# Top-32 attention and a low-rank mixer in one kernel: a fold's maximum read from PSUM, keys stored tail first, and weighted values at the head of a step

## The chip, the cores and the metric

The kernel runs on one core of one Trainium2 chip. The core has a matrix engine (TensorE, PE in the profile, with its weight loader PEld), three other compute engines (VectorE or DVE, ScalarE or ACT, GpSimd or POOL) and a queue engine (SyncE, SP) that issues most transfers here. Each engine runs its own instructions in order; semaphores tie them together. The metric is the time of one execution on the device in microseconds, as a median of several. For the kernel before that is 1749.21 us (three runs, 1747.92 to 1749.37).

## The reference, cut to what matters

There are 8 batches, 8 heads, 576 positions and head dimension 64, all in float32. The outputs of the heads of a batch, side by side, are the input of a mixer of 512 channels.

```python
scores = scale * np.matmul(q, k.transpose(0, 1, 3, 2))          # 576 x 576 per head
kth = np.partition(scores, -32, axis=-1)[..., -32:-31]
scores = np.where(scores >= kth, scores, -1e9)
attn = exp(scores - max) / (sum + 1e-9)
x = matmul(attn, v)                       # heads side by side: (8, 576, 512)
h = x.transpose(0, 2, 1) @ U @ V          # rank 32, over positions
u = x + h.transpose(0, 2, 1)
out = u + np.maximum(u @ w_ch1, 0.0) @ w_ch2    # 512 -> 2048 -> 512
```

The costly part outside the matrix products is the 32nd largest of 576 scores in each row.

## The kernel before, in words

**Groups and steps.** Two heads of one batch make a group g (0 to 31, four to a batch). A group has five query tiles t: four of 128 rows (t = 0 to 3, "full tiles"), in which both heads have 128 rows each, and a tail tile (t = 4) in which the last 64 rows of both heads share the 128 partitions. Step n is group n // 5, tile n % 5; there are 160. One Python loop (L753 to L866) writes out the order of all engines by hand, without a scheduler. In step n it issues the scores of step n+1, most of the top-32 search of step n, the transposes of the weights of step n-1, and the weighted values of an earlier step. Steps from 21 on use the second half of the loop's body (L830 on).

**Scores.** `scores` (L310) makes a full tile's scores in two PSUM tiles, `scs[0]` and `scs[1]`, each two banks wide: `scs[0]` has the first 288 keys of head 0 and of head 1, `scs[1]` the other 288. The products have a contraction of 64, so that the two heads use the two halves of the PE array (shown as 64*128 in the profile). The PSUM pool `ps_s` has two buffers. ScalarE copies the scores to SBUF with three instructions (L346 to L348), because in SBUF a row is [head 0: main 512, tail 64][head 1: tail 64, main 512], while the keys lie main first for both heads. `load` (L237) reads keys in that order with one transfer for the main part and one for the tail of each block. From group 5 on (`blocked`, L279) inputs are loaded in blocks of 32 and turned by VectorE's transpose (L290) rather than by PE.

**Top 32 with a fold.** From group 4 on, a row of 576 scores is folded in two halves of 288: `upper` has the larger of each pair, `lower` the smaller. GpSimd adds the two halves as integers (stage 0, L370), VectorE takes the maximum (stage 1, L372), and GpSimd subtracts it from the sum (L373), which leaves the smaller one exactly. `fold` starts this right after the scores, `split` does the second stage some way later in the same step. VectorE then looks for maxima in `lower` (L412 to L416) and in `upper` (L426, L438, L443).

**Weights and values.** After the top 32 is known, ScalarE and GpSimd drop the other scores and ScalarE takes the exponential (L377). From step 30 on the weights of a full tile are transposed by VectorE in blocks of 32 (L498) and by way of DRAM (`away`, L504, then one transfer L508 into `PT`, which has two buffers); the last piece goes through PE (L531). `values` (L541) multiplies the transposed weights with v on PE: for a full tile one product over the whole array (L560) and eight that use half the array's columns (L564, shown as 128*64), for a tail tile five over the whole array (L550). ScalarE copies the result (L573; L558 for a tail tile, after VectorE's reciprocal of the sums, L539). In step n these are the values of step n-2, in the middle of the step (L850 to L853). When a group's tail tile has had its values, `mixed` is queued for that group (transposes, the low-rank products), and after four groups the batch's MLP becomes a filler.

**Filler.** The MLP of the batch before (L633, L652: 256 products of 256 or 320 columns) fills PE during the attention of the next. `fill` (L725) is called eight times a step; each call adds a fixed share to an account `due` and issues MLP products until that is spent, or sets it to zero if no MLP is queued. For steps up to 42 the share is multiplied by 0.91 (`EARLY`). What is left of the last MLPs runs after the last step.

Of the kernel before, what the change touches and what calls it, by code (L numbers as in the profile page):

```python
# [12 lines left out]
ALU = mybir.AluOpType  # L13
# [13 lines left out]
def kernel(  # L27
# [28 lines left out]
    nc = tc.nc  # L56
    B, H, S, D = q.shape
# [5 lines left out]
    NT, TAIL = 4, 64  # L63
    MAIN = NT * P
    HALF = S // 2
# [4 lines left out]
    CH = NT + 1  # L70
    ALONE = NPAIR * CH
# [4 lines left out]
    BLK = 32  # L76
# [52 lines left out]
    def cols(t):  # L129
        return slice(t * P, t * P + rows(t))  # L130
# [4 lines left out]
    def half(h):  # L135
        return slice(h * D, (h + 1) * D)
# [77 lines left out]
    raws, parts, passes = [], [], []  # L214
# [17 lines left out]


    raw, qkTs, S2s, uTs, XTs, dens = {}, {}, {}, {}, {}, {}
    probs, PTs, folds = {}, {}, {}

    def load(g):  # L237
        b, h0 = g // NPAIR, 2 * (g % NPAIR)
        ld = loads.tile([P, 2 * S], F32, tag="ld", name="ld")
        if blocked(g):  # L240
            for i, src in enumerate((q, k)):
                for a in range(4):
                    ds = src[b, h0 + a // 2, :, a % 2 * BLK : (a % 2 + 1) * BLK]
                    to = ld[a * BLK : (a + 1) * BLK, i * S : (i + 1) * S]
                    nc.sync.dma_start(
                        to[:, 0:MAIN].rearrange("i (t m d) -> i t m d", t=NT, d=BLK),
                        ds[0:MAIN].rearrange("(m i t) d -> i t m d", i=BLK, t=NT),
                    )
                    nc.sync.dma_start(
                        to[:, MAIN:S].rearrange("i (m d) -> i m d", d=BLK),  # L250
                        ds[MAIN:S].rearrange("(m i) d -> i m d", i=BLK),
                    )
            raw[g] = ld
        else:
            tiles = []
            ends = ld[:, 2 * MAIN : 2 * S].rearrange("p (h d) -> p h d", h=2)
            for j, src in enumerate((q, k)):
                t = ld[:, j * MAIN : (j + 1) * MAIN].rearrange("p (t h d) -> p t h d", t=NT, h=2)
                for i in range(2):
                    queue = nc.scalar if g == 0 and i else nc.sync  # L260
                    queue.dma_start(
                        t[:, :, i, :],
                        src[b, h0 + i, 0:MAIN, :].rearrange("(p t) d -> p t d", t=NT),
                    )
                tiles.append(t)
            for i, src in enumerate((q, k)):
                nc.sync.dma_start(
                    ends[half(i)], src[b, h0 : h0 + 2, MAIN:S, :].rearrange("h p d -> p h d")
                )
            raw[g] = tiles, ends  # L270
        va, vd, vt = (a[g % NV] for a in (vas, vds, vts))
        for i in range(2):
            nc.sync.dma_start(
                va[:, i], v[b, h0 + i, 0:MAIN, :].rearrange("(p t) d -> p t d", t=NT)
            )
            nc.sync.dma_start(vd[half(i), half(i)], v[b, h0 + i, MAIN:S, :])
        nc.sync.dma_start(vt[TAIL:P], v[b, h0 : h0 + 2, MAIN:S, :].rearrange("h p d -> p h d"))

    def blocked(g):  # L279

        return g > NPAIR
# [26 lines left out]
    def scores(g, t):  # L310

        qkT = qkTs[g]
        S2 = attn.tile([P, 2 * (S + TAIL)], F32, tag="Ssb", name="Ssb", bufs=4)
        n = 2 if t < NT else 1
        probs[g, t] = S2
        S2s[g, t] = S2[:, 0 : n * S].rearrange("p (c n) -> p c n", c=n)
        if t == NT:
            sc = ps_s.tile([P, 2, 512], F32, tag="sc", name="sc")  # L320
            for i in range(2):
                for h in range(2):
                    nc.tensor.matmul(  # L323
                        sc[half(h), i, 0:HALF],
                        lhsT=qkT[half(h), 0, cols(t)],
                        rhs=qkT[half(h), 1, i * HALF : (i + 1) * HALF],
                        start=True,
                        stop=True,
                    )
            nc.scalar.copy(S2[:, 0:S].rearrange("p (i n) -> p i n", i=2), sc[:, :, 0:HALF])  # L330
            return
        scs = [ps_s.tile([P, 2, 512], F32, tag="sc", name="sc") for _ in range(2)]
        for i, sc in enumerate(scs):
            for h in range(2):
                nc.tensor.matmul(  # L335
                    sc[:, h, 0:HALF],
                    lhsT=qkT[half(h), 0, cols(t)],
                    rhs=qkT[half(h), 1, i * HALF : (i + 1) * HALF],
                    start=True,
                    stop=True,  # L340
                )

        main = S2.rearrange("p (h n) -> p h n", h=2)
        last = S2[:, MAIN : MAIN + 2 * TAIL].rearrange("p (h n) -> p h n", h=2)
        copy = nc.vector.tensor_copy if g + t == 0 else nc.scalar.copy
        copy(main[:, :, 0:HALF], scs[0][:, :, 0:HALF])  # L346
        nc.scalar.copy(main[:, :, HALF:MAIN], scs[1][:, :, 0 : MAIN - HALF])
        nc.scalar.copy(last, scs[1][:, :, MAIN - HALF : HALF])  # L348

    def fold(g, t):  # L350

# [11 lines left out]
    def pair(g, t, stage):  # L363
        S2 = S2s[g, t]
        n = S2.shape[1]
        upper, lower = folds[g, t]
        top, bottom = upper[:, 0:n, 0:HALF], lower[:, 0:n].bitcast(U32)
        a, b = S2[:, :, 0:HALF], S2[:, :, HALF:S]
        if stage == 0:
            nc.gpsimd.tensor_tensor(bottom, a.bitcast(U32), b.bitcast(U32), ALU.add)  # L370
        else:
            nc.vector.tensor_tensor(top, a, b, ALU.max)  # L372
            nc.gpsimd.tensor_tensor(bottom, bottom, top.bitcast(U32), ALU.subtract)  # L373

    def weigh(chunk, E, nmax, total=None):
# [165 lines left out]
    def values(g, t):  # L541

        PT = PTs.pop((g, t))
        va, vd, vt = (a[g % NV] for a in (vas, vds, vts))
        O = ps_t.tile([P, P], F32, tag="tp", name="O")
        if t == NT:
            den, x = dens[g], xs[g % 2]
            inverse(g, 2 * NT if g == NPAIR - 1 else 0, 2 * NT + 1)
            for j in range(NT + 1):
                nc.tensor.matmul(  # L550
                    O,
                    lhsT=PT[:, j],
                    rhs=va[:, :, j, :] if j < NT else vt,
                    start=(j == 0),
                    stop=(j == NT),
                )
            for h in range(2):
                nc.scalar.mul(x[half(h), NT, half(h)], O[half(h), half(h)], den[half(h), 2 * NT :])  # L558
            return
        nc.tensor.matmul(O, lhsT=vd, rhs=PT[:, 2 * NT], start=True, stop=False)  # L560
        PB = PT[:, 0 : 2 * NT].rearrange("p (a h) (c j) -> p h c a j", h=2, c=NT)
        for j in range(NT):
            for h in range(2):
                nc.tensor.matmul(  # L564
                    O[half(h)],
                    lhsT=va[:, h, j, :],
                    rhs=PB[:, h, j] if shared(g, t) else PT[:, NT * h + j],
                    start=False,
                    stop=(j == NT - 1),
                )  # L570
        if t == 0:
            XTs[g] = attn.tile([P, MAIN], F32, tag="XT", name="XT")
        nc.scalar.copy(XTs[g][:, cols(t)], O)  # L573
# [144 lines left out]
    STEPS = NP * CH  # L718
# [6 lines left out]
    def fill(k=1):  # L725


        nonlocal due
        for _ in range(k):
            if passes:  # L730
                passes.pop(0)()
            if mixing and next(mixing[0], True):
                mixing.pop(0)
            due += share * (SHORT if t == NT else 1) * (EARLY if n <= 2 * ALONE + 2 else 1)
            while due > 0:
                if not fillers:
                    due = 0.0
                    break
                done = next(fillers[0], None)
                if done is None:  # L740
                    fillers.pop(0)
                else:
                    due -= done

    load(0)
    next_params(1)
    t = 0
# [5 lines left out]
    for n in range(STEPS + 2):  # L753
# [77 lines left out]
        if ease:  # L831
            next(last, None)
        fill()
        if n + 1 < STEPS:
            scores(*divmod(n + 1, CH))
            fold(*divmod(n + 1, CH))
# [10 lines left out]
        next(here, None)  # L847
        next_params(1)
        fill()
        if n - 2 >= ALONE:  # L850
            values(*divmod(n - 2, CH))
            if (n - 2) % CH == NT:
                mixing.append(mixed((n - 2) // CH, 5))  # L853
        next(here, None)
        split(*divmod(n + 1, CH))
        if away:
# [43 lines left out]
```

## Time and profile before

| | |
|---|---|
| median of the runs | 1749.21 us |
| the profiled execution | 1745.95 us |
| its span, from first to last instruction | 1744.1 us |
| attention of groups 0 to 3, no filler yet | until about 215 us |
| attention with filler | 215 to some 1612 us |
| last batch's MLP alone | 1612 to 1744 us |
| mean clock granted to PE | 0.968 (0.78 until 215 us, 1.00 from 320 on) |
| HBM | 95 GB/s over the span |

How to read it: an engine's busy time is what its instructions cover; idle time on an engine that is not the bottleneck costs nothing, and which engine is the bottleneck differs from stage to stage. A 4-byte matrix product appears as two records on PE and two on its weight loader. The number after the shape, 64*128 or 128*64, is the part of the array that a product uses. In a line of a group, the figures after the bar are busy time, mean length of one in ns, and the engine's idle time before them with what ended it.

### The profile page before, as it was taken

Reading aid. Unit: us, or ns where it says so; the run is one execution under the profiler, and the core shown is the slowest. Engines: PE = TensorE matmul, PEld = TensorE weight load, DVE = VectorE, ACT = ScalarE, POOL = GpSimd, SP = SyncE. Lnnn points to the kernel's source line nnn. Section 1 sums busy time; section 2 is a strip of 40 time slices with the busy share of each in tenths; the row PEclk is TensorE's granted clock in tenths of the full one; section 3 lists DMA queues with packets and bytes.
Section 4 is the critical chain, followed back from the end, with each engine's and each line's share of the span. In section 5 each row is a group of like instructions: output and inputs, shape, how many; then the busy total and the mean of one; then the engine's idle time right before and its main releaser. Section 6 shows DMA issues by size and latency. Waiting matters only on the chain.

```text
span 1744.1 us, 29711 instructions
## 1 busy us (share of the span) xinstructions
PE 1638.1 (94%) x9435; PEld 1202.4 (69%) x9435; DVE 1515.5 (87%) x4358; ACT 1030.4 (59%) x2690; POOL 973.2 (56%) x759
## 2 busy tenths in 40 slices
PE   4576789999999999999999999999999999999999
PEld 2444556677667776678767776678767776678677
DVE  7999889899999999999999999999999999993000
ACT  4888787665656666565656656565656666563100
POOL 4778787656555555656555555656555555652000
PEclk7678899999999999999999999999999999999999
DMA  3332222344444443444444444444444444422010
GB/s 89 89 93 82 71 72 60 70 111 112 112 109 122 107 117 101 116 107 112 109 111 120 103 113 106 116 113 112 109 112 123 105 111 105 121 85 82 3 16 13
DMA packets 275837, 167.36 MB, mean 96 GB/s; under 512 B 173920, under 2 KB 260192, under 8 KB 275680
## 3 DMA queue, kind: packets, MB, share of 16 engines
q1 hardware_dynamic: 274624, 165.20, 36.4%
q8 instruction: 74, 1.21, 0.3%
q14 instruction: 83, 0.68, 0.1%
q10 hardware_dynamic: 1056, 0.26, 0.1%
HBM read 101.42 MB, written 63.96 MB: 95 GB/s over the span
## 4 chain that ended last, share of the span: by engine, by line
PE 73%; DVE 16%; ACT 3%; DMA 3%; POOL 3%; issue 2%; SPq 1%; POOLq 0%; DVEq 0%; ACTq 0%
PE mm L652 26%; PE mm L633 23%; PE sc L335 6%; PE O L564 6%; DVE m L443 5%; DVE hT L438 3%; DVE upper L438 2%; DMA PT<-away 2%; PE sc L323 2%; DVE first L426 2%; PE O L550 2%; PE up L608 1%; PE tp L531 1%; PE O L560 1%; PE tp L526 1%
## 5 line engine op out<-in xcount | busy, mean ns | idle before, releaser
L652 PE MATMUL mm<-hT,w 128*128 128x256 f32 (+1 forms) x2048 | 544.6, 410 | 0.7 <-ACT hT L645 0.7
L633 PE MATMUL mm<-uT,w 128*128 128x256 f32 (+1 forms) x2048 | 540.2, 411 | 0.0
L471 POOL TENSOR_TENSOR Ssb<-Ssb,E 128x576 f32<-128x576 f32 x271 | 379.4, 1418 | 270.5 <-ACT E L468 269.9
L633 PEld LDWEIGHTS mm<-uT,w 128*128 128x128 f32 x2048 | 376.1, 192 | 100.0 <-issue 13.3
L652 PEld LDWEIGHTS mm<-hT,w 128*128 128x128 f32 x2048 | 373.6, 192 | 95.2 <-issue 11.7
L443 DVE MAX8 m<-upper 128x8 f32<-128x304 f32 x756 | 323.9, 466 | 2.9
L373 POOL TENSOR_TENSOR lower<-lower,upper 128x576 uint32<-128x576 uint32 (+1 forms) x140 | 180.5, 1289 | 137.2 <-DVE upper L372 130.5
L377 ACT ACTIVATE Ssb<-Ssb,nmax 128x576 f32<-128x576 f32 x286 | 222.6, 783 | 17.2 <-POOL Ssb L448 9.2
L370 POOL TENSOR_TENSOR lower<-Ssb 128x576 uint32<-128x576 uint32 (+1 forms) x140 | 194.8, 1392 | 59.3 <-DVE first L426 18.3
L438 DVE MATCH_REPLACE8 upper<-m,upper 128x304 f32<-128x304 f32 x504 | 227.6, 459 | 0.0
L645 ACT ACTIVATE hT<-mm 128x320 f32<-128x320 f32 (+1 forms) x256 | 105.8, 413 | 201.1 <-PE mm L633 198.7
L468 ACT ACTIVATE E<-Ssb,least 128x576 f32<-128x576 f32 x271 | 197.9, 769 | 5.2
L335 PE MATMUL sc<-qkT 64*128 64x288 f32 x1024 | 167.7, 448 | 9.3 <-ACT Ssb L346 8.5
L564 PE MATMUL O<-PT,va 128*64 128x128 f32 x2048 | 144.4, 285 | 9.8 <-DMA PT<-away 9.5
L498 DVE STREAM_TRANSPOSE y<-Ssb 128x512 f32<-128x512 f32 x208 | 138.5, 694 | 8.2 <-ACT Ssb L377 7.4
L335 PEld LDWEIGHTS sc<-qkT 64*128 64x128 f32 x1024 | 91.9, 194 | 71.3 <-issue 27.8
L412 DVE MAX8 upper<-lower 128x8 f32<-128x288 f32 x252 | 103.0, 445 | 41.0 <-POOL lower L373 41.0
L372 DVE TENSOR_TENSOR upper<-Ssb 128x576 f32<-128x576 f32 (+1 forms) x140 | 123.7, 884 | 11.6 <-ACT Ssb L348 11.0
L564 PEld LDWEIGHTS O<-PT,va 128*64 128x64 f32 x2048 | 113.0, 140 | 27.0 <-DMA PT<-away 12.2
L665 DVE TENSOR_TENSOR oT<-uT,mm 128x320 f32<-128x320 f32 (+1 forms) x8 | 3.6, 455 | 140.8 <-PE mm L652 140.8
L346 ACT COPY Ssb<-sc 128x576 f32<-128x576 f32 x127 | 80.6, 635 | 71.4 <-PE sc L335 69.9
L573 ACT COPY XT<-O 128x128 f32<-128x128 f32 x128 | 34.2, 267 | 143.1 <-PE O L564 143.1
(95 smaller groups left out, 2233.8 us busy)
## 6 DMA issues: line engine op xcount, KB each, us to landing
away<-y SPq DMA_DIRECT2D x416, 128.0 KB, 2.4
PT<-away SPq DMA_DIRECT2D x104, 512.0 KB, 3.3
raw<-in_moe_w_ch_dram SPq DMA_DIRECT2D x32, 512.0 KB, 3.8
va<-in_v_dram SPq DMA_DIRECT2D x64, 128.0 KB, 2.2
out_dram<-ob SPq DMA_DIRECT2D x57, 128.0 KB, 2.0
ld<-in_q_dram SPq DMA_DIRECT2D x108, 64.0 KB, 2.6
ld<-in_k_dram SPq DMA_DIRECT2D x108, 64.0 KB, 2.3
ld<-in_q_dram SPq DMA_DIRECT2D x108, 8.0 KB, 2.2
```

Of the source, the lines that this page charges most:

```text
L335: nc.tensor.matmul(sc[:, h, 0:HALF], lhsT=qkT[half(h), 0, cols(t)], rhs=qkT[half(h), 1, i * HALF : (i + 1) * HALF], start=True, stop=True,)
L370: nc.gpsimd.tensor_tensor(bottom, a.bitcast(U32), b.bitcast(U32), ALU.add)
L373: nc.gpsimd.tensor_tensor(bottom, bottom, top.bitcast(U32), ALU.subtract)
L377: nc.scalar.activation(E, chunk, AF.Exp, bias=nmax, scale=SCALE, accum_out=total)
L438: nc.vector.match_replace(nxt, ms[c], curs[c], NEG)
L443: nc.vector.max(ms[c], curs[c])
L468: nc.scalar.activation(gap, chunks[c], AF.Relu, bias=least[:, c : c + 1], scale=-WIDEN)
L471: nc.gpsimd.tensor_tensor(chunks[c], chunks[c], gap, ALU.subtract)
L498: nc.vector.transpose(y[:, :, h].rearrange("p r c j -> p c r j"), E2[:, a : a + MAIN].rearrange("p (c r j) -> p c r j", c=NT, r=4),)
L564: nc.tensor.matmul(O[half(h)], lhsT=va[:, h, j, :], rhs=PB[:, h, j] if shared(g, t) else PT[:, NT * h + j], start=False, stop=(j == NT - 1),)
L633: nc.tensor.matmul(ph[:, 0:w], lhsT=w1[:, cc, f * P : (f + 1) * P], rhs=uT[:, cc, lo:hi], start=(cc == 0), stop=(cc == NC - 1),)
L652: nc.tensor.matmul(po[:, 0:w], lhsT=w2[:, f, c * P : (c + 1) * P], rhs=hTs[f][:, 0:w], start=(f == 0), stop=(f == NF - 1),)
```

## The change

Three things are changed together.

- For blocked groups (5 to 31) the keys of head 1 are loaded tail first: [tail 64, main 512]. Head 1's two parts of 288 are then already in the order in which SBUF has them. A full tile's `scs[0]` gets part 0 of head 0 and part 1 of head 1, `scs[1]` the other two, and ScalarE makes two copies of 2 x 288 instead of three. For the tail tile the scores keep their order, so that one of its four products becomes two (224 and 64 columns).
- The fold's maximum takes one of its two operands from the PSUM tile (`fronts_of`) and not from its copy in SBUF: for full tiles of blocked groups, and for all tail tiles. GpSimd's addition reads SBUF as before. The PSUM tile is in use until the maximum has read it.
- The values of step n-3 are issued at the head of step n, directly before the scores of step n+1, in place of those of step n-2 in the middle of the step. Only the last two steps keep the old place. `mixed` is queued from there too.

```diff
     def load(g):
...
+                    lead = TAIL if i and a >= 2 else 0
                     nc.sync.dma_start(
-                        to[:, 0:MAIN].rearrange("i (t m d) -> i t m d", t=NT, d=BLK),
+                        to[:, lead : lead + MAIN].rearrange("i (t m d) -> i t m d", t=NT, d=BLK),
                         ds[0:MAIN].rearrange("(m i t) d -> i t m d", i=BLK, t=NT),
                     )
+                    end = 0 if lead else MAIN
                     nc.sync.dma_start(
-                        to[:, MAIN:S].rearrange("i (m d) -> i m d", d=BLK),
+                        to[:, end : end + TAIL].rearrange("i (m d) -> i m d", d=BLK),
                         ds[MAIN:S].rearrange("(m i) d -> i m d", i=BLK),
                     )
...
     def scores(g, t):
...
+        def product(out, h, lo, hi):
+            nc.tensor.matmul(
+                out,
+                lhsT=qkT[half(h), 0, cols(t)],
+                rhs=qkT[half(h), 1, lo:hi],
+                start=True,
+                stop=True,
+            )
+
         if t == NT:
             sc = ps_s.tile([P, 2, 512], F32, tag="sc", name="sc")
             for i in range(2):
                 for h in range(2):
...
+                    lo = i * HALF + (TAIL if h and blocked(g) else 0)
+                    hi = min(lo + HALF, S)
+                    product(sc[half(h), i, 0 : hi - lo], h, lo, hi)
+                    if hi - lo < HALF:
+                        product(sc[half(h), i, hi - lo : HALF], h, 0, TAIL)
             nc.scalar.copy(S2[:, 0:S].rearrange("p (i n) -> p i n", i=2), sc[:, :, 0:HALF])
+            fronts_of[g, t] = sc[:, 0:1, 0:HALF]
             return
...
         for i, sc in enumerate(scs):
             for h in range(2):
...
+                part = 1 - i if h and blocked(g) else i
+                product(sc[:, h, 0:HALF], h, part * HALF, (part + 1) * HALF)
+        if blocked(g):
+            for i, sc in enumerate(scs):
+                nc.scalar.copy(ends_of(S2, i), sc[:, :, 0:HALF])
+            fronts_of[g, t] = scs[0][:, :, 0:HALF]
+            return
...
+    def ends_of(S2, i):
+
+        parts = S2[:, 0 : 4 * HALF].rearrange("p (a n) -> p a n", a=4)
+        return parts[:, 1:3] if i else parts[:, 0:4:3]
+
...
     def pair(g, t, stage):
...
         a, b = S2[:, :, 0:HALF], S2[:, :, HALF:S]
+        if t < NT and blocked(g):
+            a, b = (ends_of(probs[g, t], i) for i in range(2))
...
-            nc.vector.tensor_tensor(top, a, b, ALU.max)
+            nc.vector.tensor_tensor(top, fronts_of.pop((g, t), a), b, ALU.max)
...
+    def weighted(m):
+
+        values(*divmod(m, CH))
+        if m % CH == NT:
+            mixing.append(mixed(m // CH, 5))
...
         if ease:
             next(last, None)
         fill()
+        if ALONE <= n - 3 <= STEPS - 3:
+            weighted(n - 3)
         if n + 1 < STEPS:
             scores(*divmod(n + 1, CH))
             fold(*divmod(n + 1, CH))
...
         fill()
-        if n - 2 >= ALONE:
-            values(*divmod(n - 2, CH))
-            if (n - 2) % CH == NT:
-                mixing.append(mixed((n - 2) // CH, 5))
+        if n >= STEPS:
+            weighted(n - 2)
         next(here, None)
         split(*divmod(n + 1, CH))
```

In it `P` is 128, `S` 576, `NT` 4, `CH` 5, `MAIN` 512, `TAIL` 64, `HALF` 288, `ALONE` 20 and `STEPS` 160.

More of the change, by code (lines that the diff above doesn't have):

```diff
@@ L234 @@
     raw, qkTs, S2s, uTs, XTs, dens = {}, {}, {}, {}, {}, {}
-    probs, PTs, folds = {}, {}, {}
+    probs, PTs, folds, fronts_of = {}, {}, {}, {}
     def load(g):
@@ L322, in scores @@
                 for h in range(2):
[L323 to L329, printed above, removed]
+                    lo = i * HALF + (TAIL if h and blocked(g) else 0)
[3 more added lines that the diff above has]
+                        product(sc[half(h), i, hi - lo : HALF], h, 0, TAIL)
             nc.scalar.copy(S2[:, 0:S].rearrange("p (i n) -> p i n", i=2), sc[:, :, 0:HALF])
+            fronts_of[g, t] = sc[:, 0:1, 0:HALF]
             return
@@ L334, in scores @@
             for h in range(2):
[L335 to L341, printed above, removed]
+                part = 1 - i if h and blocked(g) else i
[5 more added lines that the diff above has]
+            return
         main = S2.rearrange("p (h n) -> p h n", h=2)
```

## The prediction

> **What bounds the kernel now.** I read the page's busy times first, then busy time by stage, then the waits and the groups by shape in the stages that matter, and last TensorE's timeline of one step with the chain of waits. The page alone leaves two candidates:
>
> ```profile
> PE 1638.1 (94%) x9435; PEld 1202.4 (69%) x9435; DVE 1515.5 (87%) x4358; ACT 1030.4 (59%) x2690; POOL 973.2 (56%) x759
> ```
>
> Busy time by stage (columns: stretch, its length, then busy time of PE, weight loader, VectorE, ScalarE, GpSimd, clock, DMA share, GB/s):
>
> ```profile
> 215.00:446.00 231.00, 214.05 (x1248) 154.79 (x1247) 217.13 (x630) 155.25 (x394) 156.92 (x121) 0.97 0.34 88
> 446.00:1577.00 1131.00, 1127.34 (x6627) 829.01 (x6627) 1082.05 (x3259) 690.40 (x1851) 656.25 (x507) 1.00 0.43 111
> 1577.00:1612.00 35.00, 34.27 (x215) 29.36 (x215) 9.86 (x26) 12.31 (x34) 8.51 (x9) 1.00 0.25 72
> 1612.00:1744.00 132.00, 126.68 (x525) 98.66 (x523) 7.03 (x15) 14.62 (x36) 0.72 (x1) 0.99 0.06 11
> ```
>
> From 446 to 1577 us PE is busy 1127.3 of 1131 and VectorE 1082: PE binds, with VectorE only 49 us behind. Before 446 PE idles 17 us and VectorE 14. After 1612 there is only the last batch's MLP on PE. A busy PE need not be a full one, so I ask who waited in the long stage (waits of PE, then of VectorE):
>
> ```profile
> PE O L564 <- DMA PT<-away: 3.3, 4, 1.9
> ...
> DVE upper L412 <- POOL lower L373: 28.7, 35, 1.3
> DVE upper L372 <- ACT Ssb L348: 7.1, 11, 0.9
> DVE y L498 <- ACT Ssb L377: 5.3, 14, 1.0
> ```
>
> PE waits for nothing but 3.3 us of a DMA. VectorE waits mostly on its own loop with GpSimd (maximum L372, subtraction L373, next maximum L412). Now one step on PE (start, length, records; a 4-byte product is two records):
>
> ```profile
> 1005.17 3.19 PE L652 MATMUL mm<-hT,w 128*128 128x256 f32 x14
> 1008.19 0.38 PE L560 MATMUL O<-PT,vd 128*128 128x128 f32 x2
> 1008.51 1.09 PE L564 MATMUL O<-PT,va 128*64 128x128 f32 x16
> 1009.53 3.72 PE L652 MATMUL mm<-hT,w 128*128 128x256 f32 x16
> 1013.18 1.24 PE L335 MATMUL sc<-qkT 64*128 64x288 f32 x8
> ```
>
> The 14 records before O take 1008.19-1005.17 = 3.02 us, 0.216 each: perfect streaming. The 16 after it take 3.65, where 16 x 0.216 = 3.45. The chain of waits has the pair side by side, the first run after O of a full tile, the second after O of the tail tile (L550, whole-array 128*128):
>
> ```profile
> 1009.60 3.65 PE mm L652 x16
> 1019.91 3.46 PE mm L652 x16
> ```
>
> So leaving the half-array O costs PE 0.19 us (3.65-3.46), with nobody waited for.
>
> **What the Trainium skill says.** "TensorEngine Tiling (Array Packing)", Key Properties: "Changing tiling mode (not just tile) drains the TensorE". The trace agrees: the 0.19 us above, at a change from 128*64 to 128*128. "TensorE: Matmul & The Clock Gate", Step-by-step: weight loads may be pulled ahead, matmuls stay in program order; so a score product that waits holds all of PE behind it. "SBUF — State Buffer", Who interferes with whom: a VectorE instruction with two SBUF inputs contends with GpSimd reads through a shared read interface, one with a single SBUF input does not. The trace agrees in part: L372 has a median of 0.745 us and a maximum of 2.008. "Perfetto Trace Analysis", Optimizing Scalar/DVE Operations, prices VectorE's access at about 60 ns for SBUF and 125 for PSUM; the trace can bound that below.
>
> **The change part by part.**
>
> *Position of the weighted values.* A full-tile step ran mm, sc, tp, mm, O, mm: it will run mm, O, sc, tp, mm. O to mm (0.19 us) disappears; mm to sc becomes O to sc. The trace shows no O next to sc. Nearest is mm to sc: the weight loader idles 0.33 us there, and I take the same toll, so the gain is 0.19. If two half-array modes followed each other without a drain it would be some 0.38; if their change cost double, zero. In the long stage steps 45 to 158 place values 42 to 155: 114, of which 23 are tail tiles (no toll before, none now), so 91 x 0.19 = 17.3 us. The 3.3 us waiting on the PT DMA go as well, since the values come half a step later than the data they used to meet. Buffers: PT has two, and the fetch of step n-1 reuses that of n-3, read at the head of step n; in the timeline the fetch is issued over 8 us after that head (996.58 for the scores at 986.68, 1004.54 for those at 995.98), so SP's queue doesn't block. It lands 3.3 us on (median of the page), at 1007.9 for the O that ran at 1008.19: just in time before, 5 us early after. On ScalarE the copy L573 (0.27 us) moves ahead of the score copies, and their O is computed before the scores they wait for. For a tail tile VectorE's reciprocal L539 (0.2 us) moves too, behind the L426 pair, with L558 of ScalarE behind it and the score copies behind that; the next maximum has 3 us or more of room there. Nothing is priced for these.
>
> *Tail tile scores.* A product is split in two: 224 and 64 columns. Two more records at the 128-column pitch of L564 (16 records, side by side in twos, in 1.02 us: 0.11 here) less 2 x 64 columns at half that: +0.11 us, 23 times: 2.5 us lost on PE.
>
> *Copies.* L346, L347, L348 (0.64, 0.54, 0.28) become two of 0.64: 0.18 us less on ScalarE, which is 61% busy in the long stage. The second ends about when the third did. Worth nothing directly.
>
> *Maximum from PSUM.* L372 by shape, in 250:446 (groups 5 on), then in 446:1577, and the only comparable operation with one PSUM input:
>
> ```profile
> L372 DVE TENSOR_TENSOR upper<-Ssb 128x576 f32<-128x576 f32 x16 | 20.0, 1252 | 0.3 <-ACT Ssb L348 0.3
> ...
> L372 DVE TENSOR_TENSOR upper<-Ssb 128x576 f32<-128x576 f32 x92 | 80.8, 878 | 7.7 <-ACT Ssb L348 7.1
> ...
> L665 DVE TENSOR_TENSOR oT<-uT,mm 128x320 f32<-128x320 f32 x4 | 2.0, 488 | 89.3 <-PE mm L652 89.3
> L665 DVE TENSOR_TENSOR oT<-uT,mm 128x256 f32<-128x256 f32 x4 | 1.7, 422 | 51.5 <-PE mm L652 51.5
> ```
>
> L665 grows 66 ns for 64 columns; at 576 it would be 488+256x1.03 = 752 ns, against 745 uncontended from SBUF. Bounds: 0.745 (PSUM free) to 0.81 (the skill's 65 ns difference on top); I take 0.755. Long stage: 92 x (0.878-0.755) = 11 us of VectorE, tail tiles 1 more. GpSimd's L370 (1549 ns on average there, 1413 for the like L373 which never overlaps a maximum) gets shorter too, and with it some of the 28.7 us at L412; say 3. VectorE's own floor falls from 1131-7 = 1124 to about 1109; PE's from 1131 to 1131-17.3-3.3+2.5 = 1113. They pass each other by 4 us: PE still binds and the stage gains 18 us. Before 446 VectorE binds (14 us idle of 231, 12.3 of it at L412): 16 x (1.252-0.755) = 8 us, of which I count 6, as a subtraction queued on GpSimd behind what caused the contention can't start earlier by all of it.
>
> *The new wait.* Score tiles come from two PSUM buffers. The first tile of a step is now held until VectorE's maximum, where ScalarE's copies freed it before. Behind a score product that waits stand the transposes and all MLP work of PE. In the long stage a maximum ends 3.3 us or more before the next scores (1008.52+1.23 = 9.75 against 13.18; 1017.75+0.74 against 23.30), and both move with the scores. I price it at zero, up to 2 us around 260 to 280 where PE ran ahead of VectorE.
>
> *The filler.* MLP products are handed out by a fixed share, and what finds no MLP left is lost until the end. As the values of group 7 come half a step later, MLP 1 opens later: in the program's own order the step after the scores of n=43 has 3 MLP products instead of 9, and after the last scores 328 instead of 320. That is 6 x 320 columns, 6 x 2 x 0.27 = 3.2 us carried into the final stage; PE can partly recover it where it is taken out, so I take 1.5, bounds 0 and 3.2.
>
> Sum: 18+6-1.5 = 22.5, so the span goes from 1744.1 to some 1722. The profiled execution took 1745.95, 1.9 us around its span and 3.3 below the median of 1749.21; the median goes to 1727.
>
> **The rivals.** (1) VectorE and GpSimd take over as the bound: L412 keeps its 28.7 us and the maximum costs 0.81. Then the long stage gains 92 x 0.07+7 = 13 us at most, less some coupling, say 9; early 4, filler -1.5: 1738. For it: floors 4 us apart. Against: L370's stretching goes for sure. (2) No drain between O and sc, or more relief at L412: the long stage gains 25 to 28 us, total 32: 1717. For it: the skill speaks of a drain per change, without a size. (3) Slower: the held score tile. VectorE's maximum of step n+1 and PE's scores of n+2 become one loop. If VectorE trails by 3.3 us more than now, every short step stalls PE; at 1 us for two steps of each of the 23 groups that is 46 us, less 22: 1773. It decides only from a trailing of 3.3 us, and PE leaving VectorE behind is just what the faster PE tends to. (4) No change: the half-array toll reappears in full between O and sc, while the floors meet: within 3 us of 1749.
>
> **How the numbers follow.** Forecast 60%, (1) 16%, (2) 11%, (3) 9%, (4) 4%. The range covers the forecast's bounds and most of (1) and (2), leaving their outer ends with (3) and (4) outside: 1714 to 1741. What a measurement here can tell from no change is 0.2%, 3.5 us. Faster: 0.86; same: 0.05; slower: 0.09.
>
> **What would show it.** The mm run after O vanishes and runs of 16 all take 3.46; the first score record follows L564's successor at about 0.2 us; the maximum has a narrow spread near 0.75; PE's wait on PT is gone; no wait of sc on VectorE above 2 us in total past 446; the step of n=43 short by 3 us. A maximum above 0.81, sc waiting on VectorE, or PE below 99% busy from 446 on would prove me wrong.

## The result, and the profile after

The changed kernel is slower: 1778.02 us (median of 4 runs, 1772.02 to 1778.22) against 1749.29 for the kernel before beside it, a ratio of 1.0157 with a 95% interval of 1.0134 to 1.0179. The profiled execution spans 1776.4 us, 32 more than before.

Busy time by engine on the page, and by stage (columns as above):

```profile
PE 1637.4 (92%) x9489; PEld 1233.3 (69%) x9489; DVE 1496.7 (84%) x4358; ACT 1020.7 (57%) x2582; POOL 957.4 (54%) x759
```

```profile
215.00:446.00 231.00, 210.54 (x1218) 157.46 (x1217) 204.78 (x617) 153.16 (x373) 155.32 (x122) 0.94 0.33 86
446.00:1577.00 1131.00, 1098.01 (x6509) 831.34 (x6509) 1048.07 (x3179) 662.31 (x1708) 626.15 (x494) 0.99 0.42 109
```

PE is busy as long as before (1637.4 against 1638.1 us), VectorE 19 us less; only the weight loader, which overlaps PE, is busy longer. In the long stage PE now idles 33 us where it idled 4, VectorE 83 where it idled 49. So something makes them wait for each other. The granted clock is lower too: 0.94 from 215 to 446 us where it was 0.97, and 0.99 in the long stage where it was 1.00. What that cost is taken up with the first experiment. The longest waits of PE, ScalarE and VectorE in the long stage (ScalarE's longest but for the ordinary ones on PE and on the top-32 result):

```profile
PE tp L602 <- ACT x L575: 31.3, 22, 2.5
PE tp L717 <- POOL oT L685: 1.7, 5, 0.3
...
ACT x L575 <- DVE den L556: 54.9, 22, 2.8
...
DVE y L515 <- ACT Ssb L394: 56.4, 69, 3.1
DVE upper L389 <- ACT Ssb L349: 9.9, 11, 1.4
```

PE's wait for the PT transfer is gone, as forecast, and it never waits for the maximum at the scores. In its place there are 22 waits of PE on ScalarE, 22 of ScalarE on one small VectorE instruction, the reciprocal of a tail tile's sums (L539 before, L556 here), and many of VectorE on the exponentials (L394). Twenty-two is one for each tail tile of the stage. Before, ScalarE waited at the same place for the product of PE, and less:

```profile
ACT x L558 <- PE O L550: 20.4, 21, 1.9
```

One of the new waits in the timeline (start, length, engine, line):

```profile
1038.98 1.05 PE L567 MATMUL O<-va,PT 128*128 128x128 f32 x8
...
1039.85 0.81 DVE L433 MAX8 upper<-lower 128x8 f32<-128x288 f32 x2
1039.87 0.39 PE L567 MATMUL O<-vt,PT 128*128 128x128 f32 x2
1040.19 1.24 PE L322 MATMUL sc<-qkT 64*128 64x288 f32 x8
1040.57 0.83 DVE L443 MAX8 first<-upper 128x8 f32<-128x304 f32 x2
...
1041.33 0.20 DVE L556 RECIPROCAL den<-den 128x9 f32<-128x9 f32 x1
...
1041.62 0.63 ACT L575 ACTIVATE x<-O,den 64x64 f32<-64x64 f32 x2 [2.49 <-DVE den L556]
...
1042.27 1.18 ACT L349 COPY Ssb<-sc 128x576 f32<-128x576 f32 x2
...
1042.30 0.66 PE L602 MATMUL tp<-ident,XT 128*128 128x128 f32 x4 [0.61 <-ACT x L575]
...
1044.13 0.78 ACT L394 ACTIVATE Ssb<-Ssb,nmax 128x576 f32<-128x576 f32 x1
```

The values' product is done at 1040.2. ScalarE has been free since 1039.1 and stands still for 2.49 us, the first 1.1 of them for the product, the rest until VectorE has worked off its searches and comes to the reciprocal. Behind the scaling L575 in ScalarE's queue are the score copies, then the exponentials; PE's mixer transposes (L602) wait for the scaling too. The chain of waits runs through this place in the same order: searches, reciprocal, scaling, mixer transposes. Of the whole chain the page puts 12% down to SP, mostly input loads (L246, L251), but VectorE is never idle before the transposes that use them (L292, 22 in the long stage, 0.0 us).

### The profile page after: what moved, and what is told of

Read it like the earlier page. It is cut to its first block, busy times and chain, and to the rows that moved or that the text cites. A ratio compares the mean times of both kernels' runs of the same rounds, so it can differ in the third digit from the quotient of the medians.

```text
span 1776.4 us, 29747 instructions
## 1 busy us (share of the span) xinstructions
PE 1637.4 (92%) x9489; PEld 1233.3 (69%) x9489; DVE 1496.7 (84%) x4358; ACT 1020.7 (57%) x2582; POOL 957.4 (54%) x759
## 4 chain that ended last, share of the span: by engine, by line
PE 52%; DVE 22%; SPq 12%; DMA 4%; ACT 4%; issue 3%; POOL 3%; DVEq 0%; POOLq 0%; ACTq 0%
PE mm L669 18%; PE mm L650 17%; DVE m L460 5%; SPq L251 5%; SPq L246 5%; PE sc L322 5%; PE O L581 4%; DVE hT L455 4%; DVE first L443 3%; DVE qkT L292 2%; DVE upper L455 2%; DVE lower L431 2%; PE up L625 2%; DMA away<-y 1%; DVE upper L433 1%
## 5 line engine op out<-in xcount | busy, mean ns | idle before, releaser
L650 PE MATMUL mm<-uT,w 128*128 128x256 f32 (+1 forms) x2048 | 526.9, 409 | 0.0
L669 PEld LDWEIGHTS mm<-hT,w 128*128 128x128 f32 x2048 | 384.2, 194 | 97.2 <-issue 7.9
L650 PEld LDWEIGHTS mm<-uT,w 128*128 128x128 f32 x2048 | 382.8, 193 | 98.0 <-issue 4.5
L387 POOL TENSOR_TENSOR lower<-Ssb 128x576 uint32<-128x576 uint32 (+1 forms) x140 | 181.8, 1298 | 150.5 <-DVE upper L455 59.5
L394 ACT ACTIVATE Ssb<-Ssb,nmax 128x576 f32<-128x576 f32 x286 | 221.4, 777 | 17.1 <-POOL Ssb L465 10.1
L322 PE MATMUL sc<-qkT 64*128 64x288 f32 x1334 | 210.5, 439 | 8.2 <-ACT Ssb L356 7.4
L515 DVE STREAM_TRANSPOSE y<-Ssb 128x512 f32<-128x512 f32 x208 | 145.2, 705 | 66.5 <-ACT Ssb L394 63.6
L322 PEld LDWEIGHTS sc<-qkT 64*128 64x128 f32 x1334 | 115.7, 183 | 63.2 <-issue 24.7
L349 ACT COPY Ssb<-sc 128x576 f32<-128x576 f32 x216 | 127.5, 642 | 32.5 <-PE sc L322 31.8
L429 DVE MAX8 upper<-lower 128x8 f32<-128x288 f32 x252 | 102.3, 442 | 15.1 <-POOL lower L390 15.0
L455 DVE MATCH_REPLACE8 upper<-first,upper 128x304 f32<-128x304 f32 x252 | 113.9, 459 | 0.0
L389 DVE TENSOR_TENSOR upper<-sc,Ssb 128x576 f32<-128x576 f32 (+1 forms) x136 | 93.0, 683 | 22.7 <-ACT Ssb L349 11.3
```

The source lines that it names most:

```text
L322: nc.tensor.matmul(out, lhsT=qkT[half(h), 0, cols(t)], rhs=qkT[half(h), 1, lo:hi], start=True, stop=True,)
L394: nc.scalar.activation(E, chunk, AF.Exp, bias=nmax, scale=SCALE, accum_out=total)
L455: nc.vector.match_replace(nxt, ms[c], curs[c], NEG)
L515: nc.vector.transpose(y[:, :, h].rearrange("p r c j -> p c r j"), E2[:, a : a + MAIN].rearrange("p (c r j) -> p c r j", c=NT, r=4),)
L650: nc.tensor.matmul(ph[:, 0:w], lhsT=w1[:, cc, f * P : (f + 1) * P], rhs=uT[:, cc, lo:hi], start=(cc == 0), stop=(cc == NC - 1),)
L669: nc.tensor.matmul(po[:, 0:w], lhsT=w2[:, f, c * P : (c + 1) * P], rhs=hTs[f][:, 0:w], start=(f == 0), stop=(f == NF - 1),)
```

## The experiments

Three theories stand against each other. R: the reciprocal now lies behind the searches in VectorE's queue, and everyone behind ScalarE's standstill pays. S: the values ahead of the scores make copies and exponentials late in every step, whatever the reciprocal does. H: the score tile that the maximum holds keeps PE back.

Each experiment ran beside the kernel before, which had 1746.8 to 1748.3 us in these series. Differences between the experiments are of medians.

**The reciprocal alone put back** (`values` is told not to issue it, and the middle of step m+2 does):

```diff
         if n >= STEPS:
             weighted(n - 2)
+        elif n - 2 >= ALONE and (n - 2) % CH == NT and n - 2 <= STEPS - 3:
+            inverse((n - 2) // CH, 0, 2 * NT + 1)
```

> The changed kernel, with one instruction put back: VectorE's reciprocal of a tail tile's sums (L539 of the kernel before) stands again in the middle of the step, one half step ahead of the values that need it. Theory R (at the head of a step the reciprocal lies behind eight searches of VectorE; ScalarE stands still for it, the score copies and exponentials behind it come late, and PE's mixer transposes wait for ScalarE): PE's 31 us of wait at the transposes in the long stage and ScalarE's 67 us for the reciprocal go, 1725 to 1740 us. Theory H (PE is held by the score tile that the maximum still reads): nothing changes, 1770 to 1785. Theory S (values ahead of the scores make the copies and the exponentials behind them late in every step, and VectorE's block transposes wait for these): 1755 to 1775, with VectorE's 56 us of wait at the block transposes kept.

Measured: 1719.61 us, ratio 0.9842 (0.9827 to 0.9856), 5 us below what theory R had expected. Theory R holds: moving 27 instructions of 0.2 us is worth 58 us. Waits of PE, of VectorE and of ScalarE at the scaling in the long stage (ScalarE's from 446 to 1550), where none for the reciprocal is left; the lines named here stand one further down than in the change (L576 is its L575):

```profile
PE tp L718 <- POOL oT L686: 1.7, 5, 0.3
```

```profile
DVE y L515 <- ACT Ssb L394: 29.4, 53, 1.5
DVE upper L389 <- ACT Ssb L349: 6.3, 11, 0.8
```

```profile
ACT x L576 <- PE O L568: 10.4, 17, 1.1
```

PE waits for nothing worth naming and is busy 1102.28 of 1104 us from 446 to 1550. VectorE still waits 29 us for exponentials, which costs nothing now that PE binds: theory S names a real wait, and not the loss. The same place of a step in this kernel:

```profile
1001.72 1.05 PE L568 MATMUL O<-va,PT 128*128 128x128 f32 x8
...
1002.61 0.39 PE L568 MATMUL O<-vt,PT 128*128 128x128 f32 x2
...
1003.03 0.63 ACT L576 ACTIVATE x<-O,den 64x64 f32<-64x64 f32 x2 [1.15 <-PE O L568]
...
1003.73 1.18 ACT L349 COPY Ssb<-sc 128x576 f32<-128x576 f32 x2
...
1004.26 0.60 PE L603 MATMUL tp<-ident,XT 128*128 128x128 f32 x4
```

ScalarE waits for the product alone, as it must; the reciprocal had been done by 994.9.

Not all of the 58 us is waiting. The page of this kernel, whose span is 1718.1 us, has the same 9489 records on PE as the change:

```profile
PE 1616.5 (94%) x9489; PEld 1222.6 (71%) x9489; DVE 1488.6 (87%) x4358; ACT 1020.7 (59%) x2582; POOL 959.3 (56%) x759
```

Of the 58.3 us between the two spans, 37.4 are idle time of PE (139.0 less 101.6) and 20.9 are the same records taking longer. The mean granted clock was 0.958 to 0.963 in the runs of the change and 0.967 to 0.969 with the reciprocal put back. One place in the change, PE's timeline and then the window from 388 to 392 us with its clock (the third number from the right):

```profile
376.68 5.35 PE L650 MATMUL mm<-uT,w 128*128 128x256 f32 x24
...
387.63 1.12 PE L602 MATMUL tp<-ident,XT 128*128 128x128 f32 x4 [3.05 <-ACT x L575]
388.54 3.62 PE L650 MATMUL mm<-uT,w 128*128 128x256 f32 x8
```

```profile
388.00:392.00 4.00, 4.00 (x13) 3.28 (x12) 3.36 (x10) 2.30 (x6) 3.09 (x3) 0.50 0.15 54
```

Behind the wait of 3.05 us for ScalarE the clock is at half, and the filler's records come every 0.43 us instead of every 0.22. From 300 to 1600 us the change has eight such stretches, the kernel before none, and the kernel with the reciprocal put back one, around 434. So the lower clock goes with the reciprocal's place as well. Which waits bring it about was not tested: most of the 22 in the long stage were followed by none.

**Only the keys, copies and maximum** (values in the middle of the step as before):

```diff
-        if ALONE <= n - 3 <= STEPS - 3:
-            weighted(n - 3)
...
-        if n >= STEPS:
+        if n - 2 >= ALONE:
             weighted(n - 2)
```

> Keys tail first, two copies and the maximum from PSUM as changed, but the values of step n-2 in the middle of step n as before. Theory R and theory S: faster than before, 1735 to 1745, since VectorE is freed of the contention and neither the reciprocal nor the scores have moved. Theory H: slower than before, 1765 to 1780, with PE waiting at the scores for the maximum.

Measured: 1743.45 us, 0.9973 (0.9966 to 0.9980). Slightly faster, and in the long stage PE waits only for PT (4.4 us), never for the maximum. So the held score tile is no loss.

**Only the move** (`load`, `scores`, `pair` of before). Against the kernel before:

```diff
         fill()
+        if ALONE <= n - 3 <= STEPS - 3:
+            weighted(n - 3)
         if n + 1 < STEPS:
             scores(*divmod(n + 1, CH))
...
-        if n - 2 >= ALONE:
-            values(*divmod(n - 2, CH))
-            if (n - 2) % CH == NT:
-                mixing.append(mixed((n - 2) // CH, 5))
+        if n >= STEPS:
+            weighted(n - 2)
```

> Scores, keys, copies and maximum of the kernel before, with the values of step n-3 at the head of the step as changed. Theory R and theory S: slower than before, 1765 to 1795, as all of the loss is here. Theory H: faster, 1725 to 1740.

Measured: 1786.44 us, 1.0224 (1.0206 to 1.0241). All of the loss is here; theory H is out.

**Values directly behind the scores**:

```diff
-        if ALONE <= n - 3 <= STEPS - 3:
-            weighted(n - 3)
         if n + 1 < STEPS:
             scores(*divmod(n + 1, CH))
             fold(*divmod(n + 1, CH))
+        if ALONE <= n - 3 <= STEPS - 3:
+            weighted(n - 3)
```

> The changed kernel with the values of step n-3 directly behind the scores of step n+1 instead of directly ahead of them; the reciprocal stands where the change put it in VectorE's order. Theory S: scores, copies and exponentials are early again, VectorE's wait at the block transposes falls under 20 us, 1725 to 1740. Theory R: ScalarE still stands still for the reciprocal, now behind the score copies, and PE's transposes still wait for it: 1755 to 1780. Theory H: as the changed kernel, 1770 to 1785.

Measured: 1787.11 us, 1.0232 (1.0213 to 1.0250). The score copies are no longer behind the standstill, and it is slower still, 7 us beyond what R had allowed; VectorE's wait at the block transposes grew to 81.9 us (446 to 1550), where theory S had it fall under 20. But this variant is no clean test, since it changes PE's order too. From the chains of this kernel and of the change, the first product of a full tile's values, behind the scores and behind the filler:

```profile
1030.58 0.42 PE O L577 x2
```

```profile
1061.90 0.22 PE O L577 x2
```

The change of array mode that the move had saved is back: 0.2 us for some 91 full tiles, an estimate of 18 us. And ScalarE's wait for the reciprocal fell to 22.1 us while the time grew, so this kernel loses in other places as well, which weren't followed up. Against theory S speak the first experiment and the next one, in which the values stay ahead of the scores and the loss is gone.

**The reciprocal in the same step, ahead of the searches.** It goes to the head of VectorE's order, before `front` issues the eight searches (two each of L429, L431, L433, L443):

```diff
         g, t = divmod(n, CH)
+        if ALONE <= n - 3 <= STEPS - 3 and (n - 3) % CH == NT:
+            inverse((n - 3) // CH, 0, 2 * NT + 1)
         if n < STEPS:
```

> The changed kernel, with the reciprocal issued at the head of the same step as the values that need it, but ahead of the eight searches of that step in VectorE's order instead of behind them. If the loss is the wait behind those searches (theory R, some 6 to 7 us of VectorE), it goes without moving the reciprocal to another step: 1718 to 1728. If any reciprocal at the head of a step is too late, because VectorE itself trails PE there: 1745 to 1775.

Measured: 1719.62 us, 0.9836 (0.9820 to 0.9852): the same as with the reciprocal a half step sooner. The place in the queue decides, not the step. Two more kernels stand between, with `hook()` (which issues the reciprocal) inside `front`; the first:

```diff
             for c in order:
                 nc.vector.match_replace(lower[:, c], spots[0][c], lower[:, c], NEG)
+            hook()
             for c in order:
                 nc.vector.max(spots[1][c], lower[:, c])
```

> The reciprocal at the head of the same step behind four of the eight searches of VectorE (some 1.8 us earlier than in the change, and 1.8 us later than ahead of all of them, with the waits between them on top). If the price follows how long ScalarE stands still, 27 times and then through both PE's wait and the late exponentials, it is between the two: 1730 to 1755. If there is a threshold, because ScalarE reaches its scaling only when the first four searches are done: 1719 to 1725.

> The same behind six of the eight searches, 0.85 us earlier than in the change. Proportional price: 1755 to 1772. Threshold: 1725 to 1760.

| searches ahead of the reciprocal | time, us | over the first row | ScalarE's wait for it, 446 to 1550 | PE busy, us | PE idle, us |
|---|---|---|---|---|---|
| 0 | 1719.62 | 0 | 0 | 1614.3 | 102.3 |
| 4 | 1729.53 | 9.9 | 17.4 | 1619.4 | 107.7 |
| 6 | 1748.04 | 28.4 | 31.4 | 1623.3 | 121.7 |
| 8 (the change) | 1778.02 | 58.4 | 54.9 | 1637.4 | 139.0 |

The last two columns are of the whole profiled execution, idle being its span less the busy time. With none and with four ahead ScalarE waits at the scaling for the product besides, 10.9 and 6.5 us.

From the waits of ScalarE and PE with six ahead (446 to 1550; L583, L563 and L610 are L575, L556 and L602 of the change):

```profile
ACT x L583 <- DVE den L563: 31.4, 17, 2.1
```

```profile
PE tp L610 <- ACT x L583: 15.5, 17, 1.7
```

The ratios of the two between are 0.9905 (0.9890 to 0.9919) and 1.0006 (0.9999 to 1.0013). Neither a step nor a straight line: the first 17 us of standstill cost some 10, the next 14 cost 18.5, the last 23.5 cost 30. In the last row 14.1 us of the difference are PE's records taking longer, at the lower clock seen above; its idle time grows by 17.3 us, in the row before by 14.0. The time for six is below what "proportional" had expected and fits the threshold's numbers; the one for four lies between the two, 0.5 us below the one range and 4.5 above the other.

**The mixer's first transposes two fillers later, reciprocal as changed** (`later` is true for the groups that wait five fillers for the product behind the transposes; they now wait three, so that it keeps its place):

```diff
         X = xs[g % 2]
+        for _ in range(2 * later):
+            yield
         tp = ps_t.tile([P, NT, P], F32, tag="tp", name="tp")
...
-        for _ in range(wait):
+        for _ in range(wait - 2 * later):
             yield
```

> The changed kernel with the reciprocal where the change put it, but with the mixer's first transposes two fillers later, so that PE has other work in the gap (its product then follows two fillers sooner, to stand where it stood). Theory R-PE (the loss is PE's own wait at these transposes, 31 us in the long stage): 1725 to 1745. Theory R-ACT (the loss is ScalarE's standstill of 2.5 us for each tail tile, which makes the exponentials late for VectorE's block transposes, and so VectorE late for the next one): 1760 to 1780, with the wait of PE gone and that of VectorE kept.

Measured: 1754.46 us, 1.0035 (1.0022 to 1.0048), between the two. Waits of VectorE and ScalarE, 446 to 1550:

```profile
DVE y L515 <- ACT Ssb L394: 42.3, 64, 1.5
```

```profile
ACT x L575 <- DVE den L556: 54.9, 22, 2.8
```

PE's wait for the scaling at these transposes falls from 43.7 to 3.0 us (215 to 1550) and 23.6 us of the 58.4 come back; ScalarE's standstill is unchanged. So PE's wait at the transposes, with the lower clock behind it, is worth some 24 us as this edit leaves it: on the page PE idles 14.6 us less than in the change and is busy 9.1 less. The other 35 us remain with ScalarE's standstill, but not all of them need come from it, since PE has new short waits at the moved transposes and the product behind them (4.9 and 4.8 us from 446 to 1550). How the 35 divide among late exponentials, late score copies and these was not tried. That L602 waits for the scaling because it takes over the PSUM buffer of the values (the pool has two, with L548 between) is read from the code and fits; no run shows it by itself.

**The move with the reciprocal in the middle of the step, scores and maximum of before** (the third experiment with the edit of the first):

```diff
         if n >= STEPS:
             weighted(n - 2)
+        elif n - 2 >= ALONE and (n - 2) % CH == NT and n - 2 <= STEPS - 3:
+            inverse((n - 2) // CH, 0, 2 * NT + 1)
```

> Scores, keys, copies and maximum of the kernel before; values of step n-3 at the head of the step; the reciprocal in the middle of the step before. This is the saved change of PE's array mode alone. If the toll is 0.19 to 0.20 us for 91 steps of the long stage, as in the prediction, and VectorE can follow: 1727 to 1734. If VectorE, still with two inputs from SBUF, can't follow: 1735 to 1745.

Measured: 1726.28 us, 0.9875 (0.9861 to 0.9890). The move alone, with the reciprocal in its old place, is worth about 22 us: the saved change of PE's array mode, and PE's waits for PT, which were 8.8 us from 215 to 1550 and are gone.

**The next MLP opened sooner** (on top of the first experiment; the last group of a batch waits three fillers instead of five before its product):

```diff
-            mixing.append(mixed(m // CH, 5))
+            mixing.append(mixed(m // CH, 3 if m // CH % NPAIR == NPAIR - 1 else 5))
```

> As the kernel with the reciprocal put back (1719.6 us), and the mixer products of the last group of a batch two fillers sooner, so that the next MLP opens sooner: 324 MLP products after the last scores instead of 328, which are 4 x 2 x 0.27 = 2.2 us at the most. If the final stage pays for every product that is carried into it: 1717 to 1718.5. If PE recovers where they are missing: 1719 to 1721.

Measured: 1725.59 us, 0.9871 (0.9856 to 0.9886): 6 us slower than with 5, outside both expected ranges. Four products fewer were carried over and the stage after the last scores became 0.8 us shorter (171.9 against 172.7), but the stretch from the scores of step 46 to those of step 159 takes 5.3 us longer. One wait of PE doubled, from 4.5 us (215 to 1550) to

```profile
PE tp L718 <- POOL oT L686: 9.1, 6, 2.8
```

which accounts for most of it. Why it grew was not followed up; opening an MLP at another point of a step shifts all its later pieces against the attention.

## Why the prediction was wrong

The forecast was 1727 us, faster by 22; the change measured 1778, slower by 29. The step that failed stands under "Position of the weighted values": "For a tail tile VectorE's reciprocal L539 (0.2 us) moves too, behind the L426 pair, with L558 of ScalarE behind it and the score copies behind that; the next maximum has 3 us or more of room there. Nothing is priced for these." The queue was named rightly, and only one of those who wait in it was asked after, the next maximum. The others were ScalarE (54.9 us of waiting at the scaling from 446 to 1550, where 10.4 are left with the reciprocal put back), PE's transposes behind its scaling (31.3 us), and VectorE's block transposes behind the exponentials (56.4 us, of which 29.4 are left). Behind PE's waits came the lower clock, which stands nowhere in the prediction. With all that priced at zero, 58 us were missing. None of the rivals was this mechanism: rival (3) had the right sign, but in the long stage the held score tile never made PE wait, and theory H fell with the second and third experiments. Of the prediction's own signs of being wrong one came true: PE was busy 97% of the long stage.

The other terms can be checked in the kernel with the reciprocal put back. Start of the scores of step 46, of step 159, and end, from the timelines:

| us | step 46 | from 46 to 159 | from 159 to the end |
|---|---|---|---|
| before | 463.3 | 1110.7 | 170.1 |
| changed | 468.1 | 1135.8 | 172.5 |
| reciprocal put back | 454.0 | 1091.4 | 172.7 |
| move and reciprocal, no PSUM | 460.9 | 1091.1 | 173.3 |

- Long stage: 18 us forecast, 19.3 measured. The kernel with the move alone has as much (1091.1), so the maximum adds nothing here, where PE binds. The toll between O and the filler is gone. PE's timeline of a step with the reciprocal put back:

```profile
1023.66 0.38 PE L578 MATMUL O<-PT,vd 128*128 128x128 f32 x2
1023.97 1.09 PE L582 MATMUL O<-PT,va 128*64 128x128 f32 x16
1025.00 1.24 PE L322 MATMUL sc<-qkT 64*128 64x288 f32 x8
1026.17 0.33 PE L548 MATMUL tp<-ident,Ssb 128*128 128x128 f32 x1
1026.34 5.01 PE L651 MATMUL mm<-uT,w 128*128 128x320 f32 x18
1031.18 0.38 PE L578 MATMUL O<-PT,vd 128*128 128x128 f32 x2
```

  O takes 1.03 us to the scores and these 1.17 to the transpose, as O took 1.02 to the filler and the scores 1.17 before; the 18 filler records then stream at 0.269 each with nothing lost. O to scores costs one change, as assumed; rivals (2) and (4) had it otherwise.
- Tail tile scores: 0.11 us forecast, some 0.01 measured (from the scores of a tail tile to the next instruction 1.13 us, 1.12 before). The 2.5 us weren't lost. The sum behind 0.11 doesn't come out as written either: two records at 1.02/16 us, less twice half of that, are 0.06.
- Maximum from PSUM, all full tiles of groups 5 on in the changed kernel, from the groups by shape:

```profile
L389 DVE TENSOR_TENSOR upper<-sc,Ssb 128x576 f32<-128x576 f32 x108 | 80.2, 743 | 12.1 <-ACT Ssb L349 11.3
```

  743 ns, and the same with the reciprocal put back. 752 to 755 was assumed, and the bound of 0.81 was not needed. The Trainium skill's rule that a VectorE instruction with one SBUF input doesn't contend with GpSimd ("SBUF — State Buffer", Who interferes with whom) is borne out: in the long stage the mean falls from 878 ns to this, and GpSimd's addition from 1549 to 1414. The surcharge of 65 ns that the prediction took for its bound from the skill's figures ("Perfetto Trace Analysis", Optimizing Scalar/DVE Operations) doesn't show against the uncontended 745 from SBUF. Before step 46 it gives 6.9 us (460.9 to 454.0), where 6 was counted; the move adds 2.4 there.
- Filler: 1.5 taken of 0 to 3.2, 2.6 measured in the final stage. The eight products left over (the prediction's sum had six of 320 columns) were 256 columns wide (16 records of 0.216, 3.5 us), less a wait of 0.7 for PT that is gone.

Without the reciprocal the sum would have been off by a few us: span 1744.1 to 1718.1, 26 us, where 22.5 was forecast.

## What to carry to other kernels

When a step is moved, list for each of its instructions the engine's queue at the new place and everyone behind the one who waits, and price each of them, small instructions too. Here 0.2 us on VectorE behind eight searches cost 58 us, and the fix is to issue it ahead of them. The best version measured is the change with the reciprocal issued early, at either place: 1719.6 us, 0.984 of the kernel before. And a wait of PE can cost more than its length: here 37 us of idle time came with 21 us of slower work.

## What was not expected of the hardware

The same 9489 records of PE took 20.9 us longer in the change than with the reciprocal put back, as the granted clock fell to half for some microseconds behind some of PE's waits (0.50 from 388 to 392 us, behind a wait of 3.05). A 64-column product beside the other head's 288-column one was nearly free (some 0.01 us), and the fp32 maximum with one input in PSUM ran at 743 ns against 745 from SBUF. A product over the whole array took 0.2 us more directly behind the scores, which use the array in halves, than behind the filler (0.42 against 0.22 for its two records).
